# Two transformer layers on one core: the order of the keys' side beside the first layer's last second product

## The chip, the core and the metric

The kernel runs on one core of one Trainium2 chip. Its time is the device time of one execution in microseconds. Engines in the profile's rows: PE is TensorE's matrix multiply, PEld its weight load, DVE VectorE, ACT ScalarE, POOL GpSimd, SP the engine whose queue issues nearly all DMAs.

## The reference

One sequence of S = 2048 rows of D = 576 float32 values goes twice through the same attention block A and the same dense block B, with one set of weights each.

```python
def A(x, wqkv, w_phi, wo):                       # 32 heads of 18
    q, k, v = heads of x @ wqkv
    pq, pk = q @ w_phi, k @ w_phi                # per head, 18 x 18
    phi_q = concat(softmax(pq), softmax(-pq))    # phi_k the same way
    kv = phi_k^T v;  z = sum of phi_k over the sequence
    return (phi_q kv / (phi_q z + 1e-6)) @ wo
def B(x, w1, b1, w2, b2):                        # F = 4608
    return relu(x @ w1 + b1)**2 @ w2 + b2
x = x + A(layernorm(x)); x = x + B(layernorm(x))     # layer 1 of the reference
x = x + A(layernorm(x)); x = x + B(layernorm(x))     # layer 2
```

A layer's `kv` and `z` are sums over all rows, so no query row of a layer can be finished before every key row of that layer has been seen.

## The kernel before, in words

The 2048 rows are four blocks of 512 (`TB`), each of four tiles of 128 rows (`NT`). Operands of the products are float32 split into a high and a low part, and a product is three matmuls: high by high, low by high, high by low. Weights that serve more than once are kept in DRAM already split (`wsplit`, `kept`); `wpair(which, ...)` brings a pair of halves of 288 columns, each half in a high and a low piece of 720 KB, into tiles of the tags `whi` and `wlo`, which have two buffers each: one pair fills them.

A layer is passed in this order: a barrier (the queries of two blocks, once all keys are summed), the dense block of two single blocks (`g_mlp`), then the dense block of the other two blocks together (`g_pair`). `g_pair` has three generators. `products` does the first product of both blocks with fewer multiplications and the second product of the first of the two; it ends with `last_rows(0)`, which adds the residual and stores the rows. `seconds` does the second product of the other block: 36 groups of 128 hidden features, each group 12 matmuls of 448 columns (`by_rows`, three for each tile of rows) and 3 of 512 columns (`features`), with the weights (`load_wide`, tiles `m_pr`, `m_ps`) and the hidden values (`load_high`, `m_pg`, `m_phc`) loaded three groups ahead. It ends with `last_rows(1)`.

Beside `seconds` of the first layer runs `back_keys`, the keys' side of the second layer for the three blocks that are done: blocks 3, 2 and 0 in this order. For a block it does

1. the norm (`g_norm` with `fine=True`): for each tile the row moments on VectorE (`bn_stats`, `bn_aggr`), the power on GpSimd, and the scaling on VectorE (`apart`); then six crossings, each a set of TensorE transposes into a PSUM slot (`cross`) and the split of that slot into high and low parts by ScalarE and VectorE (`split`);
2. for blocks 3 and 2 a copy of the normalized rows to DRAM (`spill`) and v (`g_v`, `make_v`: for each tile both halves of the weights);
3. the keys: for each tile the product (`make_raw`), the two softmaxes (`soft_parts`, `soft_exp`, `soft_sums`, `soft_scale`) and, one tile later, the sums over rows (`kv_tile`).

During `seconds` five accumulators and the key sums take six of the eight PSUM banks, so transposes, v and key products share two slots of the tag `w`. The normalized rows (`xn`), the raw keys and others share five buffers of the tag `qk`.

After `seconds` comes v of block 0 (`v_prev`), the norm and keys of the last block, and the second layer's barrier.

Three things set the order. `weave(main, other, rate)` traces a step of `main`, adds `rate` to what is due, and traces steps of `other` as long as their costs (the numbers that they yield) are due. `chained` puts the VectorE, ScalarE and GpSimd instructions of each of the other's steps behind those of its step before. Then the framework that builds the program orders each engine's instructions once for all, by its own estimate of when each is ready, and in the order of tracing among those that are; `tc.issue_after(ins)` keeps what is traced inside it behind `ins` on the same engine. Each engine then runs its own list in order.

Of the kernel before, what the change touches and what calls it, by code (L numbers as in the profile page):

```python
# [15 lines left out]
NT = TB // P  # L16
# [5 lines left out]
def layers_kernel(  # L22
# [74 lines left out]
    def drain(gen):  # L97
        for _ in gen:
            pass
# [28 lines left out]

    def chained(gen):
        ends, engines = {}, (nc.vector.engine, nc.scalar.engine, nc.gpsimd.engine)  # L130
        while True:
            traced = nc.cur_bb.bb.instructions
            mark = len(traced)
            with ExitStack() as behind:
                for ins in ends.values():
                    behind.enter_context(tc.issue_after(ins))
                cost = next(gen, gen)
# [207 lines left out]

    def moved(which, half, pair, back):
        for piece, home in zip(pair, wsplit[which]):
            for p, c0, c1 in parts_of(which):
# [5 lines left out]
    def wloaded(which, half, name, tags):  # L354
        pair = piece_tiles(name, tags)
        moved(which, half, pair, False)
        return pair

    def keep_split(which, pair):
# [21 lines left out]
    def g_norm(x_of, dst, name, then=None, fine=False):  # L381
# [3 lines left out]

        def scale(t):
            x = x_of(t)
            mv, rstd = moments(x, t, name)
            if fine:
# [50 lines left out]
        if not fine:  # L440
            yield from lagged(NT, scale, turn_all)
            return
        xns, pts = {}, {}

        def apart(t):
            xns[t] = scale(t)

# [11 lines left out]

        for t in range(NT):  # L460
            apart(t)
            yield 2.2
        yield from pipeline(3 * NT // 2, (cross, split), (0.3, 0.6))

# [21 lines left out]

    def make_v(x, t, pair, name):
        vt = vslots[dense["v"] % NT]
        dense["v"] += 1
        v3 = vt[:, : H * VW].rearrange("p (h d) -> p h d", d=VW)  # L490
        for half in range(2):
            pt = project(x, t, pair[half], f"{name}pv{half}{t}")
            dense["evicted"] = nc.scalar.activation(v3[:, half * H // 2 : (half + 1) * H // 2, 1:],
                                                    pt[:, :HP].rearrange("p (h d) -> p h d", d=DH), AF.Copy)
        return vt
# [625 lines left out]
    def g_pair(layer, blocks, x, after, name):  # L1121
# [217 lines left out]
        def seconds():  # L1339
# [4 lines left out]
            for f in range(NF, 2 * NF - 1):  # L1344
                if f + 3 < 2 * NF:
                    load_wide(f + 3)
                    load_high(f + 3)
                second(f)
                yield
# [121 lines left out]
    for layer in range(2):  # L1471
# [24 lines left out]
        def back_keys():  # L1496
            new_slots("vs")
            late = []
            for b in order[:3]:
                m = f"1_{b}"  # L1500
                last = b == order[2]
                xk, vts, raws, es, rs = {}, [], {}, {}, {}
                yield from g_norm(rows_of(b), xk, f"n{m}", fine=True)
                while late:
                    kv_tile(1, *late.pop(0))
                    yield 0.8
                if not last:
                    spill(b, xk)
                    yield from paced(g_v(xk, wpair("v", f"w{m}"), vts, f"v{m}"), 1.0)
                pair = wpair("k", f"w{m}")  # L1510

                def raw(t):
                    raws[t] = make_raw(xk, t, pair, f"k{m}k")

# [7 lines left out]
                def keep_sums(t):  # L1522
                    if not last:
                        late.append((vts[t], es[t], f"kv{m}_{t}"))
                        if len(late) > 1:
                            kv_tile(1, *late.pop(0))

                yield from pipeline(NT, (raw, start, lambda t: soft_exp(es[t]), end, keep_sums),
                                    (1.0, 2.6, 0.4, 1.8, 0.8))
                if last:  # L1530
# [8 lines left out]

        weave(g_mlp(layer, order[1], nxt, [], f"m{layer}_{order[1]}", None, then), back, 5.0)  # L1540
        back = iter(()) if layer else chained(back_keys())
        for k, _ in enumerate(products):
            if k == NP - 1:
                next(back, None)
                next(back, None)
        weave(seconds, back, 4.0)
        if layer == 0:
# [33 lines left out]
```

## Time and profile before

| what | value |
|---|---|
| median of 3 runs | 2533.43 us (2531.08 to 2536.16) |
| profiled execution: time | 2538.57 us |
| profiled execution: span, first to last instruction | 2536.8 us |
| mean granted TensorE clock in it | 0.992 |
| busy: TensorE, its weight loads | 2481.7 us (98%), 2179.8 us (86%) |
| busy: VectorE, ScalarE, GpSimd | 1570.9 us (62%), 1265.5 us (50%), 949.5 us (37%) |
| HBM over the span | 136 GB/s |

A row of the timeline reads: start in us, duration in us, engine, line of the kernel, operation, output and inputs by the program's names (trailing numbers left out, so `n_3p` is a PSUM tile of block 3's norm), count of instructions merged into the row, and in brackets how long the engine was idle just before and what it waited for. A row of windows gives for a stretch of time each engine's busy time and instruction count, the mean granted TensorE clock (1.00 is full speed), the share of time in which the DMA engines moved data, and GB/s.

### The profile page before, as it was taken

The page shows a single profiled execution, that of the slowest core. Times are in us where ns is not written, and L with a number is a line of the kernel's source. Part 1 is how long each engine was busy: PE and PEld are TensorE (multiplying, and loading weights), DVE is VectorE, ACT ScalarE, POOL GpSimd, SP SyncE. Part 2 cuts the span into 40 slices and gives each one's busy share as a digit, 9 for nine tenths or more (in the row PEclk, how much of TensorE's full clock was granted, in tenths as well). Part 3 has the DMA queues.
Part 4 walks back from the last instruction along what each step waited for, and adds up shares of the span by engine and source line. Part 5 has one row for each costly group of instructions (what it writes and reads, how often), then busy time and mean ns, then how long its engine had stood idle before and what let it go on. Part 6 is the DMA issues. An engine that isn't in the chain of part 4 may idle for free.

```text
span 2536.8 us, 41468 instructions
## 1 busy us (share of the span) xinstructions
PE 2481.7 (98%) x15108; PEld 2179.8 (86%) x15108; DVE 1570.9 (62%) x2514; ACT 1265.5 (50%) x2245; POOL 949.5 (37%) x1101
## 2 busy tenths in 40 slices
PE   8998999999999999999999989999999999999999
PEld 8997888889888888888889988888898888888888
DVE  6778848554856655554667679394548566555444
ACT  4344545443446666663333435454445466666642
POOL 3544312212325555551333333031123355565322
PEclk8999999999999999999999999999999999999999
DMA  9222643356434433328654134333563444333363
GB/s 326 79 69 91 196 116 85 103 164 213 133 119 125 143 114 99 113 93 295 206 180 148 47 128 150 102 99 98 166 222 112 129 130 142 116 96 109 112 199 127
DMA packets 249691, 348.52 MB, mean 137 GB/s; under 512 B 30158, under 2 KB 157262, under 8 KB 246926
## 3 DMA queue, kind: packets, MB, share of 16 engines
q1 hardware_dynamic: 248228, 343.18, 42.7%
q8 instruction: 118, 1.93, 0.3%
q10 hardware_dynamic: 1258, 2.70, 0.3%
q14 instruction: 87, 0.71, 0.1%
HBM read 279.46 MB, written 66.32 MB: 136 GB/s over the span
## 4 chain that ended last, share of the span: by engine, by line
PE 47%; DVE 3%; DMA 2%; ACT 1%; POOL 1%; issue 1%; SPq 0%; DVEq 0%; ACTq 0%; POOLq 0%
PE m_1ph L887 5%; PE m_0ph L887 4%; PE m_pacacc L1231 4%; PE m_ppx L1202 4%; PE m_1acc L914 3%; PE m_0acc L914 3%; PE m_pacc L1231 3%; PE m_ppy L1202 2%; PE m_pacacc L1221 2%; PE m_pach L1231 1%; PE m_0acc L905 1%; PE m_1acc L905 1%; PE m_pacc L1221 1%; PE m_ppz L1202 1%; PE a_0po L805 1%
## 5 line engine op out<-in xcount | busy, mean ns | idle before, releaser
L1192 POOL TENSOR_TENSOR m_ps<-m_pr,m_ps 128x128 fp32r<-128x128 f32 x144 | 118.2, 821 | 338.6 <-ACT m_ps L1190 282.9
L1191 DVE TENSOR_TENSOR m_ps<-m_pr,m_ps 128x448 fp32r<-128x448 f32 x144 | 98.1, 681 | 194.7 <-ACT m_ps L1190 191.3
L1231 PE MATMUL m_pacc<-m_ps,m_phb 128*128 128x448 f32 x864 | 188.5, 366 | 0.0
L1231 PEld LDWEIGHTS m_pacc<-m_ps,m_phb 128*128 128x128 f32 x864 | 162.2, 188 | 18.0
L1190 ACT ACTIVATE m_ps<-m_pr 128x576 fp32r<-128x576 f32 x144 | 98.1, 681 | 154.5 <-issue 88.2
L1231 PE MATMUL m_pacacc<-m_ps,m_phc 128*128 128x448 f32 x648 | 147.7, 370 | 0.0
L1231 PEld LDWEIGHTS m_pacacc<-m_ps,m_phc 128*128 128x128 f32 x648 | 122.6, 190 | 9.9
L1212 DVE TENSOR_TENSOR m_phb<-m_pz,m_phb 128x512 fp32r<-128x512 f32 x72 | 56.5, 784 | 113.1 <-ACT m_pz L1211 111.6
L914 PE MATMUL m_2acc<-m_2s,m_2hb 128*128 128x448 f32 x432 | 100.2, 366 | 0.0
L914 PE MATMUL m_0acc<-m_0s,m_0hb 128*128 128x448 f32 x432 | 100.1, 366 | 0.0
L887 PE MATMUL m_3ph<-t0onh,m_3h 128*128 128x512 f32 (+1 forms) x380 | 98.0, 383 | 1.6 <-DVE t0onh L426 0.8
L914 PE MATMUL m_1acc<-m_1s,m_1hb 128*128 128x448 f32 x432 | 99.4, 365 | 0.0
L914 PE MATMUL m_3acc<-m_3s,m_3hb 128*128 128x448 f32 x432 | 99.4, 365 | 0.0
L887 PE MATMUL m_1ph<-t1onh,m_1h 128*128 128x512 f32 (+1 forms) x380 | 97.8, 382 | 1.5 <-DVE t1onh L426 0.8
L887 PE MATMUL m_0ph<-a_0nh,m_0h 128*128 128x512 f32 (+1 forms) x380 | 97.8, 384 | 0.0
L887 PE MATMUL m_2ph<-a_2nh,m_2h 128*128 128x512 f32 (+1 forms) x380 | 97.8, 384 | 0.0
L914 PEld LDWEIGHTS m_2acc<-m_2s,m_2hb 128*128 128x128 f32 x432 | 80.9, 188 | 10.5 <-ACT m_2hb L895 0.2
L914 PEld LDWEIGHTS m_0acc<-m_0s,m_0hb 128*128 128x128 f32 x432 | 80.9, 188 | 10.6 <-ACT m_0hb L895 0.2
L914 PEld LDWEIGHTS m_1acc<-m_1s,m_1hb 128*128 128x128 f32 x432 | 81.1, 188 | 10.3
L914 PEld LDWEIGHTS m_3acc<-m_3s,m_3hb 128*128 128x128 f32 x432 | 81.1, 188 | 10.3
L872 POOL TENSOR_TENSOR m_3s<-m_3r,m_3s 128x128 fp32r<-128x128 f32 x36 | 24.6, 683 | 168.6 <-ACT m_3s L867 154.1
L872 POOL TENSOR_TENSOR m_1s<-m_1r,m_1s 128x128 fp32r<-128x128 f32 x36 | 24.7, 686 | 167.7 <-ACT m_1s L867 153.3
(2440 smaller groups left out, 7372.1 us busy)
## 6 DMA issues: line engine op xcount, KB each, us to landing
m_pr<-in_B_w SPq DMA_DIRECT2D x144, 288.0 KB
m_pr<-in_B_w SPq DMA_DIRECT2D x72, 256.0 KB
hd<-m_pu SPq DMA_DIRECT2D x72, 256.0 KB
m_pg<-hd SPq DMA_DIRECT2D x72, 256.0 KB
m_3r<-in_B_w SPq DMA_DIRECT2D x36, 288.0 KB
m_2r<-in_B_w SPq DMA_DIRECT2D x36, 288.0 KB
m_1r<-in_B_w SPq DMA_DIRECT2D x36, 288.0 KB
m_0r<-in_B_w SPq DMA_DIRECT2D x36, 288.0 KB
```

The source lines that it names most:

```text
L805: nc.tensor.matmul(pt[:, :HP], a, m[:w, g], start=(g == 0 and k == 0), stop=(g == NG - 1 and k == 2))
L872: nc.gpsimd.tensor_sub(s2[:, D + R : 2 * D], r2[:, R:], s2[:, R:D].bitcast(F32))
L887: dense["hidden"] = nc.tensor.matmul(ph[:, cols], a, m, start=(k == 0), stop=(k == len(ops) - 1))
L905: nc.tensor.matmul(acc[KC], a, m, start=(f == 0 and k == 0), stop=(f == NF - 1 and k == 2))
L914: nc.tensor.matmul(acc[t][:, :R], a[:, rows], m, start=(f == 0 and k == 0), stop=(f == NF - 1 and k == 2))
L1190: nc.scalar.activation(s2[:, :D], r2, AF.Copy)
L1191: nc.vector.tensor_sub(s2[:, D : D + R], r2[:, :R], s2[:, :R].bitcast(F32))
L1192: nc.gpsimd.tensor_sub(s2[:, D + R : 2 * D], r2[:, R:], s2[:, R:D].bitcast(F32))
L1202: nc.tensor.matmul(ps, a, m, start=start and i == 0, stop=i == len(ms) - 1, skip_group_check=True)
L1212: nc.vector.tensor_sub(hl, r, hh.bitcast(F32))
L1221: nc.tensor.matmul(accs[b][KC], a, m, start=(g == 0 and k == 0), stop=(g == NF - 1 and k == 2))
L1231: nc.tensor.matmul(accs[b][t][:, :R], a[:, rows], m, start=(g == 0 and k == 0), stop=(g == NF - 1 and k == 2))
```

## The change

No operation is added or taken away; order, waits and the pace change.

- `chained(..., strict=True)` for `back_keys`: the TensorE instructions of each step also stay behind the TensorE instruction that was traced last.
- `seconds` yields after each tile of rows and after the features, five times a group, and is woven at 0.85 instead of once a group at 4.0; step costs change (keys 0.5, 2.4, 0.4, 2.0, 0.8 for 1.0, 2.6, 0.4, 1.8, 0.8; a split 0.9 for 0.6).
- The norm's tile step is split in two stages, moments (`start`, 2.0) and scaling (`apart`, 1.6), with a step's yield between.
- v is done half by half of the weights: four tiles with half 0, then four with half 1. After each half the two pieces of that half of k's weights are loaded (`g_load`). Behind each of the first six half products one step of the next block's norm is taken.
- v's weights (block 0: k's) are loaded piece by piece, one piece a step, from the norm's seventh step in this block on; `g_load` keeps each piece on SP behind the SP instruction traced last.
- Six steps instead of two are taken ahead of `last_rows(0)`.

```diff
--- before.py
+++ after.py
@@ -126,11 +126,16 @@
         yield from (1.0 for _ in range(n))
         yield from gen
 
-    def chained(gen):
+    def traced_on(engine):
+        return next(i for i in reversed(nc.cur_bb.bb.instructions) if i.engine == engine.engine)
+
+    def chained(gen, strict=False):
         ends, engines = {}, (nc.vector.engine, nc.scalar.engine, nc.gpsimd.engine)
         while True:
             traced = nc.cur_bb.bb.instructions
             mark = len(traced)
+            if strict:
+                ends[nc.tensor.engine] = traced_on(nc.tensor)
             with ExitStack() as behind:
                 for ins in ends.values():
                     behind.enter_context(tc.issue_after(ins))
@@ -343,8 +348,9 @@
             return [(slice(0, GW), 0, NG - 1), (slice(0, gw[-1]), NG - 1, NG)]
         return [(slice(0, P), 0, NC)]
 
-    def moved(which, half, pair, back):
-        for piece, home in zip(pair, wsplit[which]):
+    def moved(which, half, pair, back, only=(0, 1)):
+        for i in only:
+            piece, home = pair[i], wsplit[which][i]
             for p, c0, c1 in parts_of(which):
                 at = half * NC * HP
                 here = piece[p, c0:c1].rearrange("p c n -> p (c n)").bitcast(F32)
@@ -355,6 +361,14 @@
         pair = piece_tiles(name, tags)
         moved(which, half, pair, False)
         return pair
+
+    def g_load(which, half, name, into):
+
+        into[half] = piece_tiles(f"{name}{which}{half}", TAGS_A)
+        for p in range(2):
+            with tc.issue_after(traced_on(nc.sync)):
+                moved(which, half, into[half], False, (p,))
+            yield 1.0
 
     def keep_split(which, pair):
         if which not in kept:
@@ -383,9 +397,12 @@
         xd = sb.tile([P, NT, 2 * 3 * TW], F32, tag="xd", name=f"{name}e", bufs=1)
         xd = xd[:, :, : 2 * DT].rearrange("p t (a d) -> p t a d", a=2)
 
-        def scale(t):
+        def begin(t):
             x = x_of(t)
-            mv, rstd = moments(x, t, name)
+            return x, *moments(x, t, name)
+
+        def scale(t, own=None):
+            x, mv, rstd = own or begin(t)
             if fine:
                 xn = sb.tile([P, D], F32, tag="qk", name=f"{name}n{t}", bufs=5)[:, : KC * P]
             else:
@@ -440,10 +457,13 @@
         if not fine:
             yield from lagged(NT, scale, turn_all)
             return
-        xns, pts = {}, {}
+        xns, pts, begun = {}, {}, {}
+
+        def start(t):
+            begun[t] = begin(t)
 
         def apart(t):
-            xns[t] = scale(t)
+            xns[t] = scale(t, begun.pop(t))
 
         def cross(i):
             if i % 3 == 2:
@@ -457,10 +477,8 @@
             else:
                 split_main(i // 3 * 2 + i % 3, pts.pop(i))
 
-        for t in range(NT):
-            apart(t)
-            yield 2.2
-        yield from pipeline(3 * NT // 2, (cross, split), (0.3, 0.6))
+        yield from pipeline(NT, (start, apart), (2.0, 1.6))
+        yield from pipeline(3 * NT // 2, (cross, split), (0.3, 0.9))
 
     def spill(b, x):
         nc.sync.dma_start(xth[b], x["h"].rearrange("p c n -> p (c n)").bitcast(F32))
@@ -484,14 +502,21 @@
             dense["projected"] = nc.tensor.matmul(pt[:, :HP], a, m, start=(k == 0), stop=(k == len(ops) - 1))
         return pt
 
-    def make_v(x, t, pair, name):
+    def next_slot():
         vt = vslots[dense["v"] % NT]
         dense["v"] += 1
+        return vt
+
+    def half_v(x, t, w, half, vt, name):
         v3 = vt[:, : H * VW].rearrange("p (h d) -> p h d", d=VW)
+        pt = project(x, t, w, f"{name}pv{half}{t}")
+        dense["evicted"] = nc.scalar.activation(v3[:, half * H // 2 : (half + 1) * H // 2, 1:],
+                                                pt[:, :HP].rearrange("p (h d) -> p h d", d=DH), AF.Copy)
+
+    def make_v(x, t, pair, name):
+        vt = next_slot()
         for half in range(2):
-            pt = project(x, t, pair[half], f"{name}pv{half}{t}")
-            dense["evicted"] = nc.scalar.activation(v3[:, half * H // 2 : (half + 1) * H // 2, 1:],
-                                                    pt[:, :HP].rearrange("p (h d) -> p h d", d=DH), AF.Copy)
+            half_v(x, t, pair[half], half, vt, name)
         return vt
 
     def new_raw(t, name):
@@ -1345,7 +1370,11 @@
                 if f + 3 < 2 * NF:
                     load_wide(f + 3)
                     load_high(f + 3)
-                second(f)
+                for t in range(NT):
+                    by_rows(f, [t], range(3))
+                    yield
+                features(f, range(3))
+                del high[f], wide[f]
                 yield
             last_rows(1)
 
@@ -1495,22 +1524,44 @@
 
         def back_keys():
             new_slots("vs")
-            late = []
-            for b in order[:3]:
+            late, ahead = [], []
+            normed = {b: {} for b in order[:3]}
+
+            def norm_of(b):
+                return g_norm(rows_of(b), normed[b], f"n1_{b}", fine=True)
+
+            norm = norm_of(order[0])
+            for i, b in enumerate(order[:3]):
                 m = f"1_{b}"
                 last = b == order[2]
-                xk, vts, raws, es, rs = {}, [], {}, {}, {}
-                yield from g_norm(rows_of(b), xk, f"n{m}", fine=True)
+                xk, vts, raws, es, rs = normed[b], [], {}, {}, {}
+                wv, wk = {}, {}
+                which, ready = ("k", wk) if last else ("v", wv)
+                loads = (cost for half in range(2) for cost in g_load(which, half, f"w{m}", ready))
+                for n, cost in enumerate(norm):
+                    yield cost
+                    if n > 5:
+                        next(loads, None)
+                drain(loads)
                 while late:
                     kv_tile(1, *late.pop(0))
                     yield 0.8
                 if not last:
                     spill(b, xk)
-                    yield from paced(g_v(xk, wpair("v", f"w{m}"), vts, f"v{m}"), 1.0)
-                pair = wpair("k", f"w{m}")
+                    norm = norm_of(order[i + 1])
+                    vts = [next_slot() for _ in range(NT)]
+                    for half in range(2):
+                        for t in range(NT):
+                            half_v(xk, t, wv[half], half, vts[t], f"v{m}")
+                            yield 0.5
+                            if len(ahead) < 6:
+                                ahead.append(t)
+                                yield next(norm)
+                        yield from paced(g_load("k", half, f"w{m}", wk), 0.3)
+                    ahead.clear()
 
                 def raw(t):
-                    raws[t] = make_raw(xk, t, pair, f"k{m}k")
+                    raws[t] = make_raw(xk, t, wk, f"k{m}k")
 
                 def start(t):
                     es[t] = soft_parts(raws.pop(t), f"k{m}K{t}")
@@ -1526,7 +1577,7 @@
                             kv_tile(1, *late.pop(0))
 
                 yield from pipeline(NT, (raw, start, lambda t: soft_exp(es[t]), end, keep_sums),
-                                    (1.0, 2.6, 0.4, 1.8, 0.8))
+                                    (0.5, 2.4, 0.4, 2.0, 0.8))
                 if last:
                     keep.update(x=xk, es=es, v=wpair("v", f"w{m}"))
 
@@ -1538,12 +1589,12 @@
             next(products)
 
         weave(g_mlp(layer, order[1], nxt, [], f"m{layer}_{order[1]}", None, then), back, 5.0)
-        back = iter(()) if layer else chained(back_keys())
+        back = iter(()) if layer else chained(back_keys(), True)
         for k, _ in enumerate(products):
             if k == NP - 1:
-                next(back, None)
-                next(back, None)
-        weave(seconds, back, 4.0)
+                for _ in range(6):
+                    next(back, None)
+        weave(seconds, back, 0.85)
         if layer == 0:
 
             prev, b = order[-2], order[-1]
```

## The prediction

> **What bounds the kernel now.** I read the page's engine totals first, then TensorE's share and clock over the one stretch that the change touches, then TensorE's rows there in order of time, then the engines and the queue behind each gap.
>
> ```profile
> span 2536.8 us, 41468 instructions
> PE 2481.7 (98%) x15108; PEld 2179.8 (86%) x15108; DVE 1570.9 (62%) x2514; ACT 1265.5 (50%) x2245; POOL 949.5 (37%) x1101
> ...
> 1163.00:1386.20 223.20, 207.71 (x1679) 190.49 (x1678) 139.42 (x201) 80.44 (x139) 75.35 (x75) 0.96 0.60 203
> ```
>
> The last row is the first layer's last second product with the keys' side woven in (columns: window, length, then busy time of TensorE, its weight loads, VectorE, ScalarE and GpSimd, then granted clock, DMA share, GB/s). TensorE bounds it, and has only two losses: idle time, 223.20 - 207.71 = 15.5 us, and clock, about 0.04 x 223 = 9 us. TensorE's rows show the idle time in four places; the 10-us windows show the clock (columns as before):
>
> ```profile
> 1173.41 0.44 PE L418 MATMUL n_3p<-ident,n_3e 128*128 128x128 f32 x2 [1.78 <-DVE n_3l L413]
> ...
> 1198.99 1.24 PE L484 MATMUL k_3kp<-w_3k0h,n_3h 128*128 128x288 f32 x5 [1.86 <-DMA w_3k0h<-wskh]
> ...
> 1252.91 0.69 PE L418 MATMUL n_2p<-ident,n_2e 128*128 128x128 f32 x2 [6.13 <-DVE n_2l L413]
> ...
> 1332.38 0.69 PE L418 MATMUL n_0p<-ident,n_0e 128*128 128x128 f32 x2 [5.55 <-DVE n_0l L413]
> ```
> ```profile
> 1170.00:1180.00 10.00, 8.09 (x50) 6.84 (x49) 7.24 (x13) 4.69 (x10) 1.90 (x3) 1.00 0.86 307
> ...
> 1190.00:1200.00 10.00, 8.14 (x54) 7.68 (x53) 0.00 (x0) 1.25 (x4) 0.00 (x0) 0.97 0.91 313
> 1200.00:1210.00 10.00, 10.00 (x60) 9.55 (x60) 2.92 (x5) 2.32 (x5) 0.90 (x1) 0.86 0.61 205
> ...
> 1250.00:1260.00 10.00, 7.05 (x88) 5.87 (x89) 6.49 (x13) 2.76 (x6) 1.28 (x2) 0.66 0.46 147
> ...
> 1320.00:1330.00 10.00, 6.82 (x37) 5.92 (x35) 7.47 (x20) 3.86 (x7) 3.64 (x8) 0.95 0.50 145
> 1330.00:1340.00 10.00, 7.62 (x95) 6.38 (x96) 7.23 (x13) 3.45 (x7) 1.44 (x4) 0.71 0.56 168
> ```
>
> Waits: 1.78 + 1.86 + 6.13 + 5.55 = 15.3 us. Clock: 10 us x (0.03 + 0.14 + 0.34 + 0.05 + 0.29) = 8.5 us. Together 23.8 us, the most that any reordering here can win.
>
> The cause of the two long waits is in VectorE's rows of block 2's norm:
>
> ```profile
> 1235.50 0.75 DVE L375 BATCH_NORM_STATS2 n_2s<-x 128x6 f32<-128x288 f32 x2
> ...
> 1240.71 0.81 DVE L375 BATCH_NORM_STATS2 n_2s<-x 128x6 f32<-128x288 f32 x2
> 1241.56 0.21 DVE L376 BATCH_NORM_AGGREGATE n_2m<-n_2s 128x2 f32<-128x12 f32 x1
> 1242.74 0.68 DVE L393 TENSOR_SCALAR n_2n<-x,n_2m,n_2d 128x512 f32<-128x512 f32 x1 [0.98 <-POOL n_2d L378]
> 1243.35 0.34 DVE L394 TENSOR_SCALAR n_2e<-x,n_2m,n_2d 128x128 f32<-128x128 f32 x1
> ...
> 1249.99 0.47 DVE L394 TENSOR_SCALAR n_2e<-x,n_2m,n_2d 128x128 f32<-128x128 f32 x1
> ...
> 1252.16 1.29 DVE L413 TENSOR_TENSOR n_2l<-n_2p,n_2h 128x512 fp32r<-128x512 f32 x2
> ```
>
> One tile takes 1240.71 to 1243.69, 2.98 us, a third of it waiting for GpSimd's power; four tiles take 1235.50 to 1250.46, 15.0 us, with the products' own VectorE work between. VectorE keeps the keys' order, so the splits of the first transposes (L413) come after all four tiles. TensorE was given far less to do meanwhile: four steps of cost 2.2 at 4.0 a group are 2.2 groups, and a group is 3.14 us:
>
> ```profile
> 1366.83 0.77 PE L1231 MATMUL m_pach<-m_ps,m_phc 128*128 128x448 f32 x3
> ...
> 1369.97 0.77 PE L1231 MATMUL m_pach<-m_ps,m_phc 128*128 128x448 f32 x3
> ```
>
> So 6.9 us of cover for 15.0 us; it meets the third transpose, whose PSUM slot L413 frees, 6.13 us too early, and every product of the stage is queued behind that transpose.
>
> **The change part by part.** No engine gets an instruction more or less: the 36 groups keep 12 + 3 matmuls, every norm, product, load and store stays. Everything below is order.
>
> Rows of block 2's norm on TensorE, VectorE and ScalarE, and two copies of v halves:
>
> ```profile
> 1244.53 1.04 PE L404 MATMUL n_2p<-ident,n_2n 128*128 128x128 f32 x8
> ...
> 1251.52 0.61 DVE L1191 TENSOR_TENSOR m_ps<-m_pr,m_ps 128x448 fp32r<-128x448 f32 x1
> ...
> 1253.37 0.68 DVE L1276 TENSOR_TENSOR m_phc<-m_pg,m_phc 128x512 fp32r<-128x512 f32 x1
> 1254.09 0.43 DVE L426 TENSOR_TENSOR n_2h<-n_2p,n_2h 64x256 fp32r<-64x256 f32 x1
> ```
> ```profile
> 1245.37 1.06 ACT L412 ACTIVATE n_2h<-n_2p 128x512 fp32r<-128x512 f32 x2
> ...
> 1264.58 0.41 ACT L493 ACTIVATE vs<-v_2pv 128x288 f32<-128x288 f32 x1 [0.59 <-PE v_2pv L484]
> 1266.42 0.41 ACT L493 ACTIVATE vs<-v_2pv 128x288 f32<-128x288 f32 x1 [1.42 <-PE v_2pv L484]
> ```
>
> *Norm in two stages, six steps of the next norm in v's products.* Tiles 0 to 2 are ready long before the transposes; only tile 3 (costs 2.0 + 1.6) stands ahead of them. 3.6 / 0.85 = 4.2 fifths of 0.63 us are 2.7 us of cover against 2.98 + 1.3 (the group's own two VectorE operations, the 0.61 and 0.68 rows) = 4.3: short by 1.6. The third transpose comes 2.4 / 0.85 = 2.8 fifths, 1.8 us, and two transposes of 0.4 us (the 1.04 us row, x8, holds two) after the first, 2.6 us, and needs half of the 1.29 us of L413 after a ScalarE copy of half of 1.06: slack 1.4. Wait left about 0.2 a block by this; I take 0.8, half way to the 1.78 row, nothing and 1.78 being the ends: 3 x 0.8 = 2.4 us.
>
> GpSimd and ScalarE in block 3's key products:
>
> ```profile
> 1210.13 1.55 POOL L524 TENSOR_TENSOR k_3K0e<-k_3K0m,k_3ks 128x576 f32<-128x576 f32 x1 [5.32 <-DVE k_3K0m L520]
> ...
> 1214.24 0.41 ACT L502 ACTIVATE k_3ks<-k_3kp 128x288 f32<-128x288 f32 x1 [0.28 <-PE k_3kp L484]
> ```
>
> The next norm holds three of the five "qk" buffers through the key products, so raw rows have two. raw(2)'s copy then needs GpSimd's L524 of tile 0: that ended at 1211.68 and raw(2)'s first copy began at 1214.24, so 2.6 us hide it; without that cover it would cost up to the 1.55 us of L524 a block. Nothing taken.
>
> *v by weight half, weights in pieces.* When today's k pieces are issued, and block 2's first use:
>
> ```profile
> 1192.64 0.32 SPq L352 DMA_DIRECT2D w_3k0h<-wskh  x1
> ...
> 1274.99 0.32 SPq L352 DMA_DIRECT2D w_2k0h<-wskh  x1
> ...
> 1280.39 0.82 PE L484 MATMUL k_2kp<-w_2k0h,n_2h 128*128 128x288 f32 x5
> ```
>
> From issue to use is 1198.99 - 1192.64 = 6.35 us in block 3 (waited for), 5.4 in block 2 (in time). In the new order half 0 is free after four v products and has the other four, with two or more groups woven, to land in: the 1.86 goes. Half 1 is now the late one: issued after the last v product, wanted 0.6 / 0.85 fifths and one half product later, by the 1.84 us from one half product's copy to the next (1264.58 to 1266.42) about 2.3 us. Where the planner, which orders each engine beforehand, foresees the landing, products stand between and nothing is lost; at worst 6.35 - 2.3 = 4 us a block. I take 1.9 for each of two blocks, the row where it was too hopeful: 3.8 us, and 1.7 us of clock with each as after that row (0.03 and 0.14 of 10 us): 3.4. A half-clock rule stands in the Trainium skill, TensorE: Matmul & The Clock Gate, "What's actually happening": the clock falls only after an idle window of about 3.4 us. The 1.86 row followed by 0.97 and 0.86 speaks against it; by the page the 3.4 would be nought and the time 2515.8.
>
> SP in block 3:
>
> ```profile
> 1146.33 0.33 SPq L352 DMA_DIRECT2D w_3v0l<-wsvl  x1
> ...
> 1162.57 3.58 SPq L1259 DMA_DIRECT2D xs<-m_px  x4
> ```
>
> The pieces are now queued on SP behind whatever was traced last: for block 3's v, behind the four stores of the last rows; and while one waits for its slot, the products' loads of three groups ahead queue behind it, 9.4 us of cover. The v pieces were issued from 1146.33; now they follow 1162.57 and its 3.58 us. With 6.35 us to land that is 1172.5 or later, and v's turn comes 2.8 groups and six sets of transposes (2 us by the 1.04 row) past the window's start at 1163, about 1174: nought taken, 4 us at worst.
>
> The issue of v's next weights, and their first use after the stage:
>
> ```profile
> 1361.40 0.32 SPq L352 DMA_DIRECT2D w_0v0h<-wsvh  x1
> ...
> 1386.22 0.82 PE L484 MATMUL v_prevpv<-w_0v0h,n_0h 128*128 128x288 f32 x5
> ```
>
> *TensorE in source order, by fifths.* The keys' steps may no longer run ahead of products traced before them; a step that waits has products behind it, as now. The supply is 35 x 5 x 0.85 = 148.8 units for steps of 139.2 (block 3: norm 10.8, v with its pieces and the next norm's six steps 16.0, keys 24.4; block 2 0.8 more; block 0 36.0; before 140 for 127), so the chain ends 11 fifths, 7 us, before the end, where it had 10 us. Block 0's last key product frees the slots of v's next weights 26 fifths (16.6 us) and the closing rows ahead of their use. Today it is 6.5 groups, 20.4 us, of the 24.8 between these two rows, so the closing rows are 4.4, and the new lead is 21 us. 6.35 us to land, four pieces, are covered: nothing. Without this cover it would cost the 6.35. Four more steps before the last rows of the first product: one tile of norm that sat beside them already: nothing.
>
> Sum: 23.8 - 2.4 - 3.8 - 3.4 = 14.2 us. The profiled execution took 2538.57 us (span 2536.8 and 1.8 around it), 5.1 over the median of 2533.43; 2538.6 - 14.2 = 2524.4 there, and 2533.4 - 14.2 = 2519.2 as a median.
>
> **The rivals.** One window of the stage with a norm in it (columns as before):
>
> ```profile
> 1240.00:1262.00 22.00, 15.84 (x135) 13.53 (x134) 14.37 (x31) 6.33 (x12) 4.67 (x10) 0.84 0.58 185
> ```
>
> *The PSUM slots decide (slower).* Transposes and splits share two slots, and with TensorE in source order each of the last four of six crossings can wait for the split two before. If each waits as 1173.41 did, 12 x 1.78 = 21.4 us; three stretches of 14.4 us, half of it these waits, at the clock of 0.84 of this row lose 6.9 more; with k's half 1 (3.8) 32.1 against 23.8 won: 2541.7. It decides from waits of 1.5 us on. For it: VectorE has 1.7 us of splits (1.29 + 0.43) and about 1.5 of product work for each 3.6 us of three crossings, and ScalarE's copies stand behind weight copies that wait. Against: the slack of 1.4 above.
>
> *The waits only move (no change).* Norm waits halve to 6.7, but each half of weights is late: half 1 by 4 us twice, block 3's v by 4, and clock stays at 8.5 less a third: 6.7 + 12 + 5.7 = 24.4 against 23.8, 2534.0. For it: 0.86 to 0.91 DMA share around block 3. Against: block 2 landed in time.
>
> *The clock falls throughout (slower).* If two cycling PSUM slots kept TensorE's clock at 0.84 over the stage, its 199.4 us of work (223.2 - 23.8) would take 237.4: 2547.6. Against it: 1.00 in 1170 to 1180, where the same cycling ran. The Trainium skill, TensorE: Matmul & The Clock Gate, "A second HAM failure mode: psum-queue depth-cycling", warns of it: frequent micro-idles make the clock oscillate. By that row the trace does not bear it out.
>
> **How the numbers follow.** Forecast 0.69; PSUM slots 0.13; waits only move 0.14; clock 0.04. Measurement tells 0.2%, 5 us, from no change. The forecast's own range goes from all 23.8 won, 2510, to the k pieces at their 4 us and the norms at 1.78 (5.3 + 8 + 3.4 = 16.7 left, 7.1 won), 2526. To leave out no more than 2 in 10 the range takes in the case of no change: 2510 to 2538. Faster 0.69, same 0.14, slower 0.17.
>
> **What would show it.** Right: no wait over 2 us before L418, clock 1.00 where 0.66 and 0.71 stood, k's half 0 without wait, a short wait for w_3k1h or w_2k1h, the stage 209 us long. Wrong: waits before L404 or L418 in most crossings; TensorE waiting for v or k pieces for 4 us; products of the weave starved of m_pr or m_pg; a wait for w_0v at the end.

## The result and the profile after

The changed kernel took 2519.45 us (median of 4 runs, 2517.46 to 2522.92), the kernel before beside it 2532.37 (2531.08 to 2536.16): a ratio of 0.9947 with the interval 0.9931 to 0.9963, 12.9 us faster. The profiled execution took 2522.92 us. Functions lie further down in the changed kernel: rest transposes L435 (L418 before), split L430 (L413), products of v and k L502 (L484), `by_rows` L1256 (L1231), `features` L1246 (L1221).

The page of the changed kernel, engine totals:

```profile
span 2521.2 us, 41458 instructions
...
PE 2477.4 (98%) x15108; PEld 2176.8 (86%) x15108; DVE 1565.9 (62%) x2514; ACT 1267.1 (50%) x2245; POOL 950.9 (38%) x1101
```

TensorE is busy 4.3 us less with the same 15108 matmuls. The span cut at the first matmul of the stage and at the first v product behind it, first the kernel before, then the changed one (window, length, busy time of TensorE, weight loads, VectorE, ScalarE, GpSimd, granted clock, DMA share, GB/s):

```profile
0.00:1163.06 1163.06, 1137.37 (x7085) 999.38 (x7086) 741.35 (x1215) 599.28 (x1077) 457.54 (x544) 0.99 0.43 135
1163.06:1386.22 223.16, 207.67 (x1679) 190.45 (x1678) 139.38 (x201) 80.44 (x139) 75.35 (x75) 0.96 0.60 203
1386.22:2536.80 1150.58, 1136.63 (x6347) 989.94 (x6345) 690.17 (x1101) 585.78 (x1029) 416.59 (x482) 1.00 0.41 127
```
```profile
0.00:1162.34 1162.34, 1137.43 (x7086) 999.73 (x7086) 743.15 (x1220) 600.13 (x1077) 458.43 (x546) 0.99 0.43 135
1162.34:1370.80 208.46, 204.19 (x1678) 187.18 (x1677) 131.88 (x195) 80.86 (x139) 74.64 (x73) 0.99 0.64 219
1370.80:2521.20 1150.40, 1135.81 (x6347) 989.88 (x6345) 690.87 (x1101) 586.12 (x1029) 417.84 (x482) 1.00 0.41 127
```

The stage went from 223.16 to 208.46: 14.7 us of the 15.6 between the two profiles. TensorE's idle time in it fell from 15.5 to 4.27 us (208.46 - 204.19), and its busy time by 3.5; the matmuls are the same to one, so that is clock. The profiles differ by more than the medians (12.9): the profiled execution of the kernel before, 2538.57, was longer than all of its timed ones, and it is the only profile of that kernel.

TensorE's rows with a wait in the changed kernel; the first lies just ahead of the stage, the others make up its 4.27 us:

```profile
1159.12 0.50 PE L1246 MATMUL m_pacc<-m_phb,m_ps 128*128 128x512 f32 x1 [1.57 <-DVE m_phb L1237]
...
1206.05 1.54 PE L502 MATMUL k_3kp<-w_3k1h,n_3h 128*128 128x288 f32 x5 [2.25 <-DMA w_3k1h<-wskh]
...
1249.52 0.44 PE L435 MATMUL n_2p<-ident,n_2e 128*128 128x128 f32 x2 [0.27 <-DVE n_2l L430]
...
1281.96 0.90 PE L502 MATMUL k_2kp<-w_2k1h,n_2h 128*128 128x288 f32 x5 [0.20 <-DMA w_2k1h<-wskh]
...
1321.85 0.44 PE L435 MATMUL n_0p<-ident,n_0e 128*128 128x128 f32 x2 [1.55 <-DVE n_0l L430]
```

Where 6.13 and 5.55 us stood there are 0.27 and 1.55. VectorE's rows of block 2's norm in the changed kernel show why:

```profile
1174.13 0.82 DVE L389 BATCH_NORM_STATS2 n_2s<-x 128x6 f32<-128x288 f32 x2
...
1176.91 0.82 DVE L389 BATCH_NORM_STATS2 n_2s<-x 128x6 f32<-128x288 f32 x2
...
1184.42 0.82 DVE L389 BATCH_NORM_STATS2 n_2s<-x 128x6 f32<-128x288 f32 x2 [1.11 <-DMA x<-xs]
...
1236.97 0.80 DVE L389 BATCH_NORM_STATS2 n_2s<-x 128x6 f32<-128x288 f32 x2
...
1239.93 0.68 DVE L410 TENSOR_SCALAR n_2n<-x,n_2m,n_2d 128x512 f32<-128x512 f32 x1 [1.92 <-POOL n_2d L392]
...
1244.54 0.69 DVE L430 TENSOR_TENSOR n_2l<-n_2p,n_2h 128x512 fp32r<-128x512 f32 x1
```

The first three tiles begin at 1174, 1177 and 1184, beside v of block 3; only the last one (1236.97) still stands between the keys of block 3 and the first split (1244.54). Before, four tiles stood there.

The stretches of 10 us with block 2's and block 0's transposes, which had a clock of 0.66 and 0.71, and the wait for k's second half with what follows it:

```profile
1206.05:1210.00 3.95, 3.95 (x16) 3.83 (x17) 0.00 (x0) 0.00 (x0) 0.00 (x0) 0.57 0.89 284
...
1240.00:1250.00 10.00, 9.73 (x56) 8.17 (x55) 8.04 (x13) 4.97 (x10) 2.13 (x3) 1.00 0.71 230
1320.00:1330.00 10.00, 8.45 (x111) 7.25 (x110) 7.23 (x12) 4.61 (x9) 1.35 (x2) 1.00 0.65 201
```

Both norms now run at full clock; the one loss left is 0.43 x 3.95 = 1.7 us behind the 2.25 us wait.

### The profile page after: what moved, and what is told of

Read it like the earlier page. It is cut to its first block, busy times and chain, and to the rows that moved or that the text cites. A ratio compares the mean times of both kernels' runs of the same rounds, so it can differ in the third digit from the quotient of the medians.

```text
span 2521.2 us, 41458 instructions
## 1 busy us (share of the span) xinstructions
PE 2477.4 (98%) x15108; PEld 2176.8 (86%) x15108; DVE 1565.9 (62%) x2514; ACT 1267.1 (50%) x2245; POOL 950.9 (38%) x1101
## 4 chain that ended last, share of the span: by engine, by line
PE 88%; DVE 4%; ACT 2%; DMA 2%; POOL 1%; issue 1%; SPq 1%; DVEq 0%; ACTq 0%; POOLq 0%
PE m_ppx L1227 8%; PE m_pacc L1256 6%; PE m_pacacc L1256 5%; PE m_1ph L912 5%; PE m_3ph L912 5%; PE m_2ph L912 5%; PE m_0ph L912 4%; PE m_ppy L1227 4%; PE m_2acc L939 3%; PE m_0acc L939 3%; PE m_1acc L939 3%; PE m_3acc L939 3%; PE m_pacacc L1246 2%; PE m_pach L1256 2%; PE m_pacc L1246 2%; PE m_ppz L1227 2%
## 5 line engine op out<-in xcount | busy, mean ns | idle before, releaser
L1256 PE MATMUL m_pacc<-m_ps,m_phb 128*128 128x448 f32 x864 | 188.5, 366 | 0.0
L1256 PEld LDWEIGHTS m_pacc<-m_ps,m_phb 128*128 128x128 f32 x864 | 162.1, 188 | 17.9
L1256 PE MATMUL m_pacacc<-m_ps,m_phc 128*128 128x448 f32 x648 | 149.6, 368 | 0.0
L1256 PEld LDWEIGHTS m_pacacc<-m_ps,m_phc 128*128 128x128 f32 x648 | 119.8, 189 | 9.1
```

The costliest lines, as they stand in the source:

```text
L1256: nc.tensor.matmul(accs[b][t][:, :R], a[:, rows], m, start=(g == 0 and k == 0), stop=(g == NF - 1 and k == 2))
```

## The experiments

The theory: the gain is the norm's. Three of its four tiles are off VectorE's list before the transposes, so TensorE's products cover the rest. The rivals: v by halves, the finer pace, or the two stages bring it; and, as a limit to all, the two PSUM slots. Diffs are against the changed kernel unless said otherwise.

**Is it the norm taken early?** The next block's norm stays where it was, all else as changed:

```diff
-                            if len(ahead) < 6:
+                            if len(ahead) < 0:
```

> The changed kernel, but no step of the next norm is taken inside v's products; the two stages, the halves of v, the fifths and the six steps ahead of block 3 stay. Theory cover (the gain is that three tiles' norms are done before the crossings begin): four tiles stand ahead of the crossings of blocks 2 and 0 again, 4 x 4.2 fifths = 10.6 us of TensorE work against the 15.0 us that they took, less 1.4 of slack: about 3 us of wait before the third transpose of each, and 1.7 of clock each: some 9 us over the changed kernel's 2519.5, 2528. Theory pace (finer weaving carries the gain): waits stay under 1.6, 2519 to 2521.

2531.43 us (10 runs), 0.9993 of before (0.9984 to 1.0003): by the medians the whole gain is gone, and the kernel is 3.4 us slower than expected. TensorE's waits in this kernel:

```profile
1243.32 0.69 PE L435 MATMUL n_2p<-ident,n_2e 128*128 128x128 f32 x2 [4.10 <-DVE n_2l L430]
...
1274.97 0.90 PE L502 MATMUL k_2kp<-w_2k1h,n_2h 128*128 128x288 f32 x5 [1.62 <-DMA w_2k1h<-wskh]
...
1326.01 0.44 PE L435 MATMUL n_0p<-ident,n_0e 128*128 128x128 f32 x2 [4.20 <-DVE n_0l L430]
```

The two norm waits are back, at 4.1 and 4.2. Its profiled execution was its shortest, 2525.92, with a stage of 216.7 us, so the kernel was profiled once more:

> The kernel with the norm back in its block once more, for a second profile: its profiled execution took 2525.9 us, the median of ten was 2531.4. If TensorE's clock makes the difference: the same two waits of about 4 us, and 3.4 to 7 us more at half clock behind them. If the waits themselves vary: waits of 6 us.

2530.07 us, a stage of 218.5, the same norm waits (4.11 and 4.20), and 2.83 for k's second half. Stage for stage these are 8.2 and 10.0 us over the changed kernel's 208.46; the medians differ by 12.0. Against the one profile of the kernel before (223.16) the two stages are still 6.5 and 4.7 us shorter, and the medians show nothing of that; that profile was of an execution 5 us over its median, so its waits may be longer than usual. What makes executions of this kernel range from 2525.92 to 2535.2 stays open: the norm waits of the two profiles are equal, and each profile lost the clock once for some 6.9 us and once for 3.4 beside them. Part of it lies outside the stage: there the first of the two profiles was 5.2 us shorter than that of the changed kernel.

**Is the norm enough by itself?** v tile by tile, one yield a group, `strict` left out; the early norm, its two stages and costs, and loads by the piece stay:

```diff
-                for t in range(NT):
-                    by_rows(f, [t], range(3))
-                    yield
-                features(f, range(3))
-                del high[f], wide[f]
+                second(f)
...
-                    for half in range(2):
-                        for t in range(NT):
+                    for t in range(NT):
+                        for half in range(2):
...
+                    for half in range(2):
                         yield from paced(g_load("k", half, f"w{m}", wk), 0.3)
...
-        back = iter(()) if layer else chained(back_keys(), True)
+        back = iter(()) if layer else chained(back_keys())
...
-        weave(seconds, back, 0.85)
+        weave(seconds, back, 4.25)
```

> Of the change only the norm's part and the loads piece by piece: the second product yields once a group (4.25), v goes tile by tile, TensorE's extra order is off. Theory cover: the norm taken early carries the gain alone, less the 1.9 us that v by tile cost: 2520 to 2523, no wait over 2 us before a third transpose. If the parts need each other: 2527 or more, waits of 3 us and more.

2519.26 us, 0.9956 (0.9942 to 0.9969), all of the gain by its median. In its profiled execution, its longest (2526.06), the stage took 211.6 us, 3.1 over the changed kernel's, with 6.7 us idle; its two longest waits are these:

```profile
1206.69 1.54 PE L502 MATMUL k_3kp<-w_3k0h,n_3h 128*128 128x288 f32 x5 [2.63 <-DMA w_3k0h<-wskh]
...
1249.86 0.44 PE L435 MATMUL n_2p<-ident,n_2e 128*128 128x128 f32 x2 [1.71 <-DVE n_2l L430]
```

**Does it have to be early, or only covered?** The kernel before with two numbers changed, so that more groups are woven beside the norm in its old place:

```diff
-            yield 2.2
+            yield 6.0
...
-        weave(seconds, back, 4.0)
+        weave(seconds, back, 5.0)
```

> The kernel before with two numbers changed: a norm tile costs 6.0 for 2.2, and the supply is 5.0 a group for 4.0. Nothing moves ahead of its block; four tiles now have 4 x 6.0 / 5.0 = 4.8 groups, 15.1 us, of TensorE work, as long as they took. Theory cover: the waits before the third transposes of blocks 2 and 0 fall under 1.5, the one for k's half 0 in block 3 stays near 1.9: 2518 to 2524. If the norm has to be done a block ahead, in v: waits of 3 us and more stay, 2528 or more.

2524.65 us (8 runs), 0.9972 (0.9963 to 0.9982): 7 of the 12.9 us, without moving a step ahead. In its profile 6.13 became 2.85, and 5.55 became 0.96:

```profile
1252.68 0.69 PE L418 MATMUL n_2p<-ident,n_2e 128*128 128x128 f32 x2 [2.85 <-DVE n_2l L413]
...
1331.39 0.44 PE L418 MATMUL n_0p<-ident,n_0e 128*128 128x128 f32 x2 [0.96 <-DVE n_0l L413]
```

Block 2's wait stayed longer than the 1.5 us expected, and the time came out just over the expected 2524. The higher supply moved other waits as well: the 1.78 us in block 3's crossings is gone, the 1.86 for k became 0.23, and 1.70 us for GpSimd, ahead of the sums over rows of block 3, is new. So cover counts, wherever it comes from; taking the steps early gave more of it.

**v by tile, all else as changed.** k's four pieces then come after the last v product:

```diff
-                    for half in range(2):
-                        for t in range(NT):
+                    for t in range(NT):
+                        for half in range(2):
...
+                    for half in range(2):
                         yield from paced(g_load("k", half, f"w{m}", wk), 0.3)
```

> The changed kernel, but v goes tile by tile with both halves of its weights again, and k's four pieces are loaded after the last v product. Theory cover: only the wait for weights changes hands, k's half 0 waits instead of half 1, 2 to 4 us a block with 1.7 of clock where a wait reaches 1.9: 2519 to 2525, norm waits as they are. Theory halves (the order of v is what frees TensorE): long waits for k in both blocks, over 2527.

2521.38 us, 0.9954 (0.9939 to 0.9969), 1.9 behind the changed kernel and within its interval. The waits stand at half 0 instead of half 1:

```profile
1202.08 0.90 PE L502 MATMUL k_3kp<-w_3k0h,n_3h 128*128 128x288 f32 x5 [1.58 <-DMA w_3k0h<-wskh]
...
1279.17 1.08 PE L502 MATMUL k_2kp<-w_2k0h,n_2h 128*128 128x288 f32 x5 [2.27 <-DMA w_2k0h<-wskh]
```

3.85 us in place of 2.45: the wait mostly moves from one half to the other, and the 1.9 us of the medians are less than these runs can tell from nothing.

**Half 0 of two tiles first.** If k's second half is the late one, the keys can begin with half 0 of tiles 0 and 1:

```diff
                 def raw(t):
-                    raws[t] = make_raw(xk, t, wk, f"k{m}k")
+                    if t < 2:
+                        half_raw(xk, t, wk, 1, raws[t], f"k{m}k")
+                    else:
+                        raws[t] = make_raw(xk, t, wk, f"k{m}k")
+
+                for t in range(2):
+                    raws[t] = new_raw(t, f"k{m}k")
+                    half_raw(xk, t, wk, 0, raws[t], f"k{m}k")
+                    yield 0.3
```

> The changed kernel, but the key products begin with half 0 of tiles 0 and 1, so half 1 of k's weights is wanted one half product (1.84 us) and a step later. If the wait for that piece (2.25 us in block 3, 0.20 in block 2) is a matter of its lead: it falls under 0.4, the 1.7 us of clock behind it goes too, about 3.7 us less, 2515.8. If the queue's backlog sets the landing and moves with it: the wait stays over 1 and the time at 2519.

2516.84 us (2516.17 to 2517.89), 0.9936 (0.9921 to 0.995). The 2.25 became 0.86, the clock was 1.00 over the stage, and the stage took 204.0 us. The wait lies between the two cases expected, the time with the first:

```profile
1204.52 0.89 PE L502 MATMUL k_3kp<-w_3k1h,n_3h 128*128 128x288 f32 x5 [0.86 <-DMA w_3k1h<-wskh]
```

**The pace, first in the changed kernel** (two of the edits of the norm's experiment, alone):

```diff
-                for t in range(NT):
-                    by_rows(f, [t], range(3))
-                    yield
-                features(f, range(3))
-                del high[f], wide[f]
+                second(f)
...
-        weave(seconds, back, 0.85)
+        weave(seconds, back, 4.25)
```

> The changed kernel, but the second product yields once a group and is woven at 4.25 for 0.85 a fifth; all else stays. Theory cover: the cover per step is the same, the planner still splits groups where it finds something ready; 2518 to 2523 and no wait over 2.5 us. Theory pace: steps come in bunches of four, the splits of a norm fall behind TensorE, waits of 3 us and more before the third transposes: 2526 or more.

2519.23 us, 0.9944 (0.9927 to 0.9961), the changed kernel's time.

**And fifths alone, in the kernel before:**

```diff
-                second(f)
-                yield
+                for t in range(NT): by_rows(f, [t], range(3)); yield
+                features(f, range(3)); del high[f], wide[f]; yield
...
-        weave(seconds, back, 4.0)
+        weave(seconds, back, 0.8)
```

> The kernel before with the second product yielding five times a group and woven at 0.8 for 4.0; nothing else. Theory cover: a norm tile still has 2.2 / 0.8 = 2.75 fifths, 1.7 us, so the waits of 5 to 6 us stay: 2529 to 2535. Theory pace: 2525 or less.

2530.84 us (10 runs), 0.9997 (0.9988 to 1.0006). The norm waits only shrink to 4.57 and 4.71. Fifths bring nothing that these runs can tell, with the early norm or without.

**The norm in one stage**, three steps of it ahead instead of six:

```diff
-        yield from pipeline(NT, (start, apart), (2.0, 1.6))
+        for t in range(NT):
+            start(t)
+            apart(t)
+            yield 3.6
...
-                    if n > 5:
+                    if n > 2:
...
-                            if len(ahead) < 6:
+                            if len(ahead) < 3:
...
-                for _ in range(6):
+                for _ in range(3):
```

> The changed kernel, but a tile's moments and scaling are one step again (cost 3.6; three steps of the next norm in v, three ahead of block 3). Theory cover: only how early the tiles are done counts; 2518 to 2521, the same waits. If the two stages count because VectorE has other work during GpSimd's power (0.98 us a tile): the tile ahead of the crossings takes 1 us longer, waits of 1 to 2.5 us in blocks 2 and 0, 2521 to 2525.

2516.83 us (2515.54 to 2518.28), 0.9941 (0.9928 to 0.9955): the two stages bring no gain, and in the profiled execution k's second half landed in time.

**Fewer steps ahead of the last rows**, with half 0 first (the diff is against that kernel). The wait ahead of the stage, 1.57 us in the changed kernel and 1.25 with half 0 first, is block 3's third norm tile, drawn there by the six steps; the hidden values of the first product queue behind it on VectorE (rows of the changed kernel):

```profile
1155.41 0.82 DVE L389 BATCH_NORM_STATS2 n_3s<-x 128x6 f32<-128x288 f32 x2 [1.64 <-DMA x<-xs]
...
1158.39 0.68 DVE L1237 TENSOR_TENSOR m_phb<-m_pz,m_phb 128x512 fp32r<-128x512 f32 x1
```
```diff
-                for _ in range(6):
+                for _ in range(4):
```

> The kernel that begins with half 0 of two tiles (2516.8), with four steps ahead of the last rows of the first product for six. The wait of 1.57 us of the last features for m_phb stands behind the third tile's moments, which wait for their rows from DRAM; with that tile after the last rows it goes: 1.3 us less, 2515.5. If the tile then falls between TensorE and block 3's crossings: up to 1.8 us before their third transpose, 2517.

2519.79 us (5 runs, 2514.43 to 2522.33), 0.9948 (0.9936 to 0.9961): no gain over half 0 first alone. It lies above both cases expected, and why stays open. The wait is gone, and another has appeared, for the last rows:

```profile
1165.71 0.67 PE L1256 MATMUL m_pacacc<-m_ps,m_phc 128*128 128x448 f32 x2 [0.66 <-DVE m_px L1282]
```

**One stage and half 0 first together** (both edits above):

> The kernel with moments and scaling in one step, and the key products beginning with half 0 of two tiles. If the late half of k's weights still cost the one-stage kernel something in executions that were not profiled: 2515 to 2516. If not: 2516.8 as each of the two alone, within 1.

2517.61 us (5 runs, 2512.81 to 2520.64), 0.9943 (0.9929 to 0.9956). Its profiled stage is the shortest of all, 202.5 us with 0.5 idle, but its median shows no gain over either edit alone. Half 0 first and one stage, both 2516.8, are the best versions found: 2.6 us below the changed kernel, which is within the 5 us that the prediction named as what a measurement can tell.

**Do the two PSUM slots limit?** The crossings paced three times as fast:

```diff
-        yield from pipeline(3 * NT // 2, (cross, split), (0.3, 0.9))
+        yield from pipeline(3 * NT // 2, (cross, split), (0.1, 0.3))
```

> The changed kernel with the crossings at a third of their pace (0.1 and 0.3 for 0.3 and 0.9): 0.9 fifths, 0.6 us, between a transpose and the one that reuses its PSUM slot, plus two transposes of 0.4, against the 1.2 us that copy and split take. Theory slots (two PSUM slots in TensorE's own order set the price): waits of 0.5 to 1.5 us at 6 to 12 crossings, 2524 to 2535. Theory planner (it lays products where it foresees a taken slot): no wait over 2 us, 2518 to 2522.

2521.05 us, 0.9956 (0.9941 to 0.9971). Its longest crossing wait, and the clock around it:

```profile
1240.52 0.44 PE L435 MATMUL n_2p<-ident,n_2e 128*128 128x128 f32 x2 [0.65 <-DVE n_2l L430]
```
```profile
1235.00:1250.00 15.00, 14.35 (x149) 12.70 (x148) 10.48 (x22) 6.05 (x12) 2.95 (x6) 1.00 0.75 267
```

Even at that pace the slots cost 1.3 us in all (0.65, 0.38 and 0.30), and cycling them did not lower the clock here.

`strict` was not run by itself: without it the changed kernel builds to the very same program, so it changes no order here. Loads by the piece were not taken out by themselves either. The kernel with the norm in place keeps them and shows no gain by its median, and the kernel with more cover has none of them and gains 7 us, so they are not the cause.

## Why the prediction was right, step by step

- *What bounds, and the cause.* Right, and shown: by the medians the norm left in place takes the gain away, the norm alone brings all of it, and more cover in the old place about half.
- *23.8 us to win at most.* Too much. The 8.5 us of clock were counted over whole windows, time in which TensorE stood idle included. Before's two waits and the clock within them:

```profile
1250.40:1252.90 2.50, 0.00 (x0) 0.00 (x0) 2.47 (x6) 0.00 (x0) 0.00 (x0) 0.53 0.54 146
...
1329.00:1332.40 3.40, 0.02 (x1) 0.03 (x1) 2.92 (x6) 0.00 (x0) 2.12 (x4) 0.51 0.44 117
```

  0.47 x 2.50 + 0.49 x 3.40 = 2.8 us of the clock loss fell into waits that were already counted. The loss was 15.5 + 5.7 = 21.2.
- *9.6 us left over.* Also too much, by about as much. Norm waits: 2.4 taken, 1.82 found (none in block 3, 0.27, 1.55). k's half 1: 3.8 taken, 2.45 found (2.25 and 0.20). Clock: 3.4 taken, 1.7 found, as block 2's wait was only 0.20. Together 4.27 + 1.7 = 6.0. So 21.2 - 6.0 = 15.2 against 14.7 measured in the stage: the forecast of 14.2 was that close because two errors of about 3 us cancelled, which is luck. So is the match of the median (2519.2 forecast, 2519.45 measured): the medians differ by 12.9, not 14.2, and the kernel before came out 1.1 us lower beside the changed one.
- *Two readings of rows.* The 1.04 us row, x8, holds two sets of transposes of 0.52 us each, not 0.4, and six sets are about 3 us, not 2. By this the slack in the norm's term is 1.6 us instead of 1.4 and v's turn comes at 1175 instead of 1174; no term of the sum changes.
- *The half-clock rule.* By the Trainium skill, TensorE: Matmul & The Clock Gate, "What's actually happening", a wait of 2.25 us leaves the clock alone; the row of 0.57 behind it says otherwise, as the row behind 1.86 did before. But the 1.7 us do not come with every wait of this length either, as the last section shows.
- *k's second half is the late one.* Right. From issue to use it took 1206.05 - 1198.99 = 7.06 us, where 6.35 was assumed. The time from its issue until it was wanted was 7.06 - 2.25 = 4.8 us, twice the 2.3 assumed, which is why the wait did not come near 4. In block 2 the piece took 4.4 us and was all but in time. SP's queue in the changed kernel:

```profile
1151.91 0.43 SPq L358 DMA_DIRECT2D w_3v0h<-wsvh  x1
...
1154.50 0.43 SPq L358 DMA_DIRECT2D w_3v0l<-wsvl  x1
...
1155.04 0.36 SPq L358 DMA_DIRECT2D w_3v1h<-wsvh  x1
...
1161.63 2.51 SPq L1284 DMA_DIRECT2D xs<-m_px  x4
...
1164.68 0.69 SPq L358 DMA_DIRECT2D w_3v1l<-wsvl  x1
...
1198.99 0.32 SPq L358 DMA_DIRECT2D w_3k1h<-wskh  x1
```

- *v's pieces follow the stores of the last rows.* Wrong for three of the four: the third, `w_3v1h`, was issued 6.6 us ahead of the stores, and only `w_3v1l` after them. A piece is tied to the one SP instruction traced last, not to the whole queue, and that can be a load which goes early. It cost nothing, as was taken.
- *Four more steps ahead of the last rows cost nothing.* Half right: a wait of 1.57 appeared, but the time ahead of the stage fell by 0.7 us all the same, and the experiment without that wait gained nothing.
- *TensorE in source order by fifths, nothing.* Right: the pace is worth nothing with the early norm or without, and no wait for `w_0v` came at the end. The source order itself was never put to the test, as `strict` changed nothing in the program.
- *The rivals.* The PSUM slots were priced at 1.78 us for each of twelve crossings; one had 1.55, and at triple pace none over 0.65. The waits did move for the weights (2.25 at half 1 for 1.86 at half 0), but not for the norms. The clock did not fall throughout.

## What to carry to other kernels

Where an in-order engine has a block of work with round trips in it (here four norm tiles of 2.98 us, a third of each spent waiting for GpSimd), compare its length with the work that the bounding engine has queued ahead of its own need; then move tiles of it early, or weave more beside it, whichever is simpler. One cause carried this change: v by halves, fifths and two stages brought little or nothing that the runs can tell, and source order changed nothing, so each part of a change is worth a run alone. When idle time and clock are both counted as losses, count the clock only where the engine was busy.

## What the runs showed of the hardware that was not expected

The half clock came in pieces of about 3.4 us: 0.43 x 3.95 / 0.5 = 3.4 behind the 2.25 us wait. With the norm in place, second profile, the two norm waits of 4.1 and 4.2 us had one such piece (0.17 x 10 / 0.5 = 3.4) and two (0.23 x 15 / 0.5 = 6.9):

```profile
1240.00:1250.00 10.00, 5.89 (x26) 4.86 (x25) 7.97 (x13) 3.00 (x6) 3.04 (x5) 0.83 0.71 215
...
1325.00:1340.00 15.00, 10.85 (x109) 9.63 (x110) 9.53 (x16) 4.38 (x8) 1.83 (x3) 0.77 0.67 218
```

The length of a wait does not decide alone whether a piece comes. In the kernel with one yield a group in place of the fifths a wait of 2.57 us at 1285 was followed by one:

```profile
1280.00:1295.00 15.00, 12.43 (x71) 11.59 (x70) 4.72 (x6) 3.44 (x7) 2.07 (x2) 0.89 0.29 101
```

Yet 2.05 us at 1209 of the same profile left the clock at 1.00, and so did 2.83 us at 1278 in the second profile of the kernel with the norm in place; 1.86 us in the kernel before did not. What they differ in is how much of the wait falls into one window of a fixed grid. In every profile here the clock changes only in steps of one grid of 3.41 us, in the kernel before at 1199.34, 1202.75, 1250.55 (15 steps after the first) and 1329.05 (23 more). The time around these waits, cut at the grid of each profile: 1.86 us in the kernel before, 2.05 with one yield a group, 2.83 with the norm in place:

```profile
1195.93:1199.34 3.41, 1.55 (x9) 1.15 (x9) 0.00 (x0) 0.00 (x0) 0.00 (x0) 1.00 0.98 363
1199.34:1202.75 3.41, 3.41 (x14) 3.13 (x13) 0.00 (x0) 0.00 (x0) 0.00 (x0) 0.50 0.87 358
```
```profile
1204.25:1207.67 3.42, 3.09 (x18) 2.60 (x16) 0.00 (x0) 0.41 (x1) 0.00 (x0) 1.00 0.79 265
1207.67:1211.08 3.41, 1.69 (x11) 1.68 (x12) 0.00 (x0) 0.00 (x0) 0.00 (x0) 1.00 0.99 365
1211.08:1214.49 3.41, 3.41 (x26) 3.30 (x25) 1.96 (x3) 1.72 (x4) 0.90 (x1) 1.00 0.42 145
```
```profile
1273.53:1276.95 3.42, 1.76 (x13) 1.38 (x11) 0.00 (x0) 0.41 (x1) 0.00 (x0) 1.00 0.83 283
1276.95:1280.36 3.41, 2.24 (x14) 2.21 (x15) 0.00 (x0) 0.00 (x0) 0.00 (x0) 1.00 0.24 98
1280.36:1283.77 3.41, 3.41 (x26) 3.28 (x25) 2.03 (x4) 1.79 (x4) 1.00 (x2) 1.00 0.02 5
```

The 1.86 us lie in one window, and the next one runs at half clock; the other two waits are shared between two windows, with at most 3.41 - 1.69 = 1.72 us in one. In the stage, over all profiles of this case, every full-clock window with 1.86 us or more of idle TensorE was followed by one at half clock, and none with 1.72 or less; a second piece followed where the half-clock window itself had 1.0 us or more idle. So where the grid happens to lie against a wait, which differs between executions of the same kernel, decides whether a wait of 2 to 3 us costs 1.7 us more. Outside the stage idle time alone does not draw the border so cleanly: one window with 1.50 us idle was followed by half clock (1496 in the changed kernel), one with 1.88 us was not (1452 in the kernel with the norm in one stage). The exact rule stays open.

The Trainium skill, TensorE: Matmul & The Clock Gate, "What's actually happening", has a window of about 3.4 us that runs freely, and these traces agree with it, by the grid of 3.41 us. Its idle window is of that whole length; here 1.86 us of idle time in one window were enough.
